# Moving each unit's predicated copy into the next unit on VectorE, and fewer masks on GpSimd, in the last tile of a fused attention and two-layer kernel

## The chip, the cores and the metric

The kernel runs on one core of a Trainium2 chip. The metric is the time of one execution on the device in microseconds (us); of the kernel before there are three runs, and one further execution was taken with the profiler.

## What is computed

Channel attention over two batches of 6016 tokens with 256 channels, then a gated layer, then a second layer with its own nonlinearity. Cut to what matters:

```python
def _moe2_ref(x, w_in, w_out):          # x: 12032 x 256, w_in: 256 x 2048, w_out: 2048 x 256
    h = x @ w_in
    g = h - np.tanh(h)
    return (g @ w_out).astype(np.float32)
```

Before it, `_attn_ref` normalises q and k along the tokens, forms a 256 x 256 softmax for each batch and applies it to v, and `_moe_ref` computes `(sigmoid(x @ w_gate) * (x @ w_val)) @ w_out`. The change touches only how `h - tanh(h)` is worked out for the last tokens.

## The kernel before, in words

**Tiles and units.** The tokens are cut into 24 tiles of up to 512 (`token_tiles`; `NT` is 24). Work comes in units: kind 1 is one of 12 slices of the gated layer of a tile, kind 2 is one of 16 slices (`K2`) of 128 hidden channels of the second layer of a tile. The list `units` is sorted by a due time. All units of kind 1 are over before the 16 units of kind 2 of the last tile (`i == NT - 1`, tile 23) begin, so those 16 follow one another with nothing between them.

**A unit of kind 2** has three parts. `s2_mm` computes the hidden values H of 128 channels in a PSUM bank (six matmuls: weights and values are split into a high and a low half, and three of the four products are taken). `s2_a` computes s = H - tanh(H). `part_b` splits s into halves: a cast on ScalarE (line 564) and a subtraction (line 566) that runs on GpSimd for the late units (`late`), on VectorE for the very last one. `part_c` multiplies the halves with the output weights (six matmuls, lines 469, 470, 474).

**The nonlinearity** in the last tile, for unit m: ScalarE computes u = H squared (line 531), d = tanh(H) (line 532) and s = (scaled u plus a bias) squared (line 533). VectorE computes e = H - d into a PSUM bank (line 543), H = H * u (line 544), s = (s + constant) * H (line 549): a polynomial that is exact enough for small H. A mask `big` says where u is over a limit, and there VectorE's predicated copy (line 550) puts e in the place of s. The mask is made by GpSimd (line 546) where m % 3 is not 0 and m is below 14, otherwise by ScalarE (line 548): nine on GpSimd, seven on ScalarE.

**Order.** Every engine works through its own queue in the order in which the program issues its instructions. In the loop over units at the end of the kernel, unit m issues `part_a` (its matmuls, then `s2_a`), then `step_b`, which is `part_b` of unit m-1, and then `part_c` of unit m-3 (`LAG` is 3). So ScalarE's queue for unit m is: square, tanh, square with bias, the mask if it is ScalarE's, the cast of unit m-1. VectorE's queue for unit m is: subtract, multiply, fused add-multiply, predicated copy. GpSimd's is: the mask if it is GpSimd's, the subtraction of unit m-1. TensorE's is: the hidden matmuls of unit m, the output matmuls of unit m-3. In unit 2 of the last tile the output matmuls and the two output copies (line 594) of tile 22 come between the unit's hidden matmuls and its `s2_a`.

**Buffers.** u, d, the mask and e have two buffers each, s has two for even and two for odd units, the PSUM ring of H has four banks, the halves (`hl`) have four.

Of the kernel before, what the change touches and what calls it, by code (L numbers as in the profile page):

```python
# [12 lines left out]
I16 = mybir.dt.int16  # L13
# [9 lines left out]
K1, K2 = F1 // P, F2 // P  # L23
# [43 lines left out]
def attn_moe_kernel(  # L67
# [12 lines left out]
    nc = tc.nc  # L80
# [15 lines left out]
    def bank(tag, name):  # L96
        return pp.tile([P, CH], F32, tag=tag, name=name)
# [423 lines left out]
    def late(i, m):  # L521
        return i == NT - 2 and m >= LATE or i == NT - 1 and m < K2 - 1

    def s2_a(i, m):
        n = tiles[i][3]
        H = live[2, i, m][:, :n]
        u = m2.tile([P, NM], F32, tag="u", bufs=2, name=f"u{i}_{m}")[:, :n]
        d = m2.tile([P, NM], F32, tag="d", bufs=2, name=f"d{i}_{m}")[:, :n]
        s = (yp if m % 2 and (i == NT - 1 or late(i, m)) else m2).tile([P, NM], F32, tag="s", bufs=2, name=f"s{i}_{m}")[:, :n]
        big = m2.tile([P, NM], BF16, tag="big", bufs=2, name=f"big{i}_{m}")[:, :n]  # L530
        nc.scalar.activation(u, H, AF.Square)  # L531
        nc.scalar.activation(d, H, AF.Tanh)  # L532
        nc.scalar.activation(s, u, AF.Square, scale=C_S, bias=c_b[:, 0:1])  # L533
        if i < NT - 1:
            nc.scalar.activation(big, u, AF.Relu, bias=c_m[:, 0:1])  # L535
            nc.vector.tensor_sub(d, H, d)  # L536
            w = H if late(i, m) else u
            nc.vector.tensor_mul(w, H, u)  # L538
            nc.vector.scalar_tensor_tensor(s, s, C_D, w, op0=ALU.add, op1=ALU.mult)  # L539
            nc.vector.copy_predicated(s, big.bitcast(I16), d)  # L540
        else:
            e = bank(f"y{m % 2}", f"e{m}")[:, :n]
            nc.vector.tensor_sub(e, H, d)
            nc.vector.tensor_mul(H, H, u)
            if m % 3 and m < K2 - 2:
                nc.gpsimd.tensor_scalar(big, u, U_MAX, 1.0, op0=ALU.is_gt, op1=ALU.mult)
            else:
                nc.scalar.activation(big, u, AF.Relu, bias=c_m[:, 0:1])
            nc.vector.scalar_tensor_tensor(s, s, C_D, H, op0=ALU.add, op1=ALU.mult)
            nc.vector.copy_predicated(s, big.bitcast(I16), e)  # L550
        live[2, i, m] = s

    def part_a(u, between=lambda: None):

        (s1_mm if u[1] == 1 else s2_mm)(*u[2:])
        between()
        (s1_a if u[1] == 1 else s2_a)(*u[2:])
# [296 lines left out]
```

## Time and profile before

| | us |
|---|---|
| median of three runs | 2313.92 |
| range of the three runs | 2313.4 to 2314.68 |
| the profiled execution's own time | 2314.18 |
| its span, first to last instruction | 2312.4 |
| busy in the span: TensorE | 2300.1 |
| busy in the span: VectorE | 1814.1 |
| busy in the span: ScalarE | 1577.3 |
| busy in the span: GpSimd | 81.2 |

In the rows below PE is TensorE, DVE is VectorE, ACT is ScalarE and POOL is GpSimd. L550 is line 550 of the kernel before. A row of a timeline has the start in us from the span's start, the duration in us, the engine, the line, the operation, what it writes and reads by the program's names, and its count; in square brackets stands how long the engine was idle before it and which instruction ended that. Durations are those of the instruction: two neighbours on one engine that do not depend on each other can overlap, so the distance of their starts is what counts. A row of stretches gives for each engine how many us of the stretch it was busy, then the granted clock of TensorE (1.00 is the higher of its two levels, 2.4 GHz), then the share and rate of the DMA engines.

### The profile page before, as it was taken

Reading aid. Unit: us, or ns where it says so; the run is one execution under the profiler, and the core shown is the slowest. Engines: PE = TensorE matmul, PEld = TensorE weight load, DVE = VectorE, ACT = ScalarE, POOL = GpSimd, SP = SyncE. Lnnn points to the kernel's source line nnn. Section 1 sums busy time; section 2 is a strip of 40 time slices with the busy share of each in tenths; the row PEclk is TensorE's granted clock in tenths of the full one; section 3 lists DMA queues with packets and bytes.
Section 4 is the critical chain, followed back from the end, with each engine's and each line's share of the span. In section 5 each row is a group of like instructions: output and inputs, shape, how many; then the busy total and the mean of one; then the engine's idle time right before and its main releaser. Section 6 shows DMA issues by size and latency. Waiting matters only on the chain.

```text
span 2312.4 us, 28293 instructions
## 1 busy us (share of the span) xinstructions
PE 2300.1 (99%) x10416; PEld 1927.1 (83%) x10416; DVE 1814.1 (78%) x2882; ACT 1577.3 (68%) x2872; POOL 81.2 (4%) x63
## 2 busy tenths in 40 slices
PE   9999999999999999999999999999999999999998
PEld 7888888888888888888899988888888888888886
DVE  5778888888888888877777777877777778777778
ACT  7567777677676767766666666666666666666667
POOL 5000000000000000000000000000000000000017
PEclk9999999999999999999999999999999999999999
DMA  9640001110101101011110000000000000000000
GB/s 341 237 134 8 23 19 37 37 37 19 37 28 32 37 19 37 0 35 35 55 37 17 10 8 19 1 19 10 10 19 10 10 19 1 19 10 10 10 1 19
DMA packets 39530, 84.65 MB, mean 37 GB/s; under 512 B 4064, under 2 KB 17376, under 8 KB 37856
## 3 DMA queue, kind: packets, MB, share of 16 engines
q1 hardware_dynamic: 38352, 76.30, 9.9%
q0 software_dynamic: 896, 6.29, 0.7%
q8 instruction: 81, 1.33, 0.2%
q14 instruction: 57, 0.47, 0.1%
q10 hardware_dynamic: 144, 0.26, 0.0%
HBM read 63.96 MB, written 18.87 MB: 36 GB/s over the span
## 4 chain that ended last, share of the span: by engine, by line
PE 94%; DVE 3%; DMA 1%; ACT 1%; issue 0%; SPq 0%; DVEq 0%; ACTq 0%
PE ps L470 11%; PE ps L469 11%; PE ps L474 11%; PE h L470 7%; PE o L474 7%; PE h L474 7%; PE h L469 7%; PE o L469 7%; PE o L470 7%; PE y L470 5%; PE y L469 5%; PE y L474 5%; DMA rawk<-in_k_dram 1%; PE aw L314 0%; PE aw L315 0%; PE aw L316 0%
## 5 line engine op out<-in xcount | busy, mean ns | idle before, releaser
L470 PE MATMUL ps<-vhl,aw 128*128 128x512 f32 (+1 forms) x1152 | 443.6, 385 | 0.0
L469 PE MATMUL ps<-vhl,aw 128*128 128x512 f32 (+1 forms) x1152 | 443.3, 385 | 0.0
L536 DVE TENSOR_TENSOR d<-h,d 128x512 f32<-128x512 f32 (+1 forms) x368 | 249.5, 678 | 235.1 <-ACT d L532 234.7
L564 ACT CAST hl<-s 128x512 fp32r<-128x512 f32 (+1 forms) x384 | 234.8, 612 | 275.1 <-DVE s L540 267.7
L531 ACT ACTIVATE u<-h 128x512 f32<-128x512 f32 (+1 forms) x384 | 226.5, 590 | 241.1 <-PE h L474 240.8
L474 PE MATMUL ps<-vhl,aw 128*128 128x512 f32 (+1 forms) x1152 | 349.8, 385 | 0.0
L538 DVE TENSOR_TENSOR u<-h,u 128x512 f32<-128x512 f32 (+1 forms) x360 | 243.5, 676 | 111.2 <-ACT big L535 111.1
L469 PE MATMUL o<-hl,wv 128*128 128x512 f32 (+1 forms) x768 | 295.8, 385 | 1.5 <-ACT hl L564 1.4
L470 PE MATMUL h<-yhl,wi 128*128 128x512 f32 (+1 forms) x768 | 295.7, 385 | 0.0
L469 PE MATMUL h<-yhl,wi 128*128 128x512 f32 (+1 forms) x768 | 295.6, 385 | 0.0
L470 PE MATMUL o<-hl,wv 128*128 128x512 f32 (+1 forms) x768 | 295.5, 385 | 0.0
L540 DVE COPY_PREDICATED s<-big,d 128x512 f32<-128x512 int16 (+1 forms) x368 | 272.8, 741 | 13.1
L533 ACT ACTIVATE s<-u,c_b 128x512 f32<-128x512 f32 (+1 forms) x384 | 275.2, 717 | 2.0 <-DVE hl L566 2.0
L535 ACT ACTIVATE big<-u,c_m 128x512 bf16<-128x512 f32 (+1 forms) x368 | 262.2, 712 | 0.0
L539 DVE SCALAR_TENSOR_TENSOR s<-s,u 128x512 f32<-128x512 f32 (+1 forms) x360 | 245.0, 681 | 12.3
L470 PEld LDWEIGHTS ps<-vhl,aw 128*128 128x128 f32 x1152 | 216.4, 188 | 40.8
L474 PEld LDWEIGHTS ps<-vhl,aw 128*128 128x128 f32 x1152 | 215.7, 188 | 41.5
L469 PEld LDWEIGHTS ps<-vhl,aw 128*128 128x128 f32 x1152 | 216.4, 188 | 40.5
L510 DVE TENSOR_TENSOR sg<-ps,sg 128x512 f32<-128x512 f32 (+1 forms) x288 | 194.3, 675 | 70.7 <-PE ps L474 55.0
L566 DVE TENSOR_TENSOR hl<-s,hl 128x512 fp32r<-128x512 f32 (+1 forms) x361 | 241.6, 669 | 0.7 <-ACT hl L564 0.7
L509 ACT ACTIVATE sg<-ps 128x512 f32<-128x512 f32 (+1 forms) x288 | 169.9, 590 | 98.0 <-PE ps L474 93.5
L474 PE MATMUL o<-hl,wv 128*128 128x512 f32 (+1 forms) x768 | 234.6, 387 | 1.8 <-POOL hl L566 1.5
(172 smaller groups left out, 3573.7 us busy)
## 6 DMA issues: line engine op xcount, KB each, us to landing
vraw<-in_vT_dram SPq DMA_DIRECT2D x22, 512.0 KB, 3.8
out_dram<-out SPq DMA_DIRECT2D x43, 256.0 KB, 2.2
raw_wgv<-in_wgv_dram SPq DMA_DIRECT2D x12, 512.0 KB, 6.7
wgv_d<-wgv POOLq DMA_DIRECT2D x6, 1024.0 KB, 7.3
wb<-wgv_d SPq DMA_DIRECT2D x6, 1024.0 KB, 4.8
raw<-in_q_dram SPq DMA_DIRECT2D x47, 128.0 KB, 2.1
raw<-in_k_dram SPq DMA_DIRECT2D x47, 128.0 KB, 2.2
rawq<-in_q_dram SPq DMA_DIRECT2D x8, 512.0 KB, 9.9
```

Of the source, the lines that this page charges most:

```text
L469: mm(ps[:, :n], wh, xh, start=first and j == 0, stop=False)
L470: mm(ps[:, :n], wl, xh, start=False, stop=False)
L474: mm(ps[:, :n], wh, xl, start=False, stop=last and j == len(wts) - 1)
L531: nc.scalar.activation(u, H, AF.Square)
L533: nc.scalar.activation(s, u, AF.Square, scale=C_S, bias=c_b[:, 0:1])
L535: nc.scalar.activation(big, u, AF.Relu, bias=c_m[:, 0:1])
L536: nc.vector.tensor_sub(d, H, d)
L538: nc.vector.tensor_mul(w, H, u)
L539: nc.vector.scalar_tensor_tensor(s, s, C_D, w, op0=ALU.add, op1=ALU.mult)
L540: nc.vector.copy_predicated(s, big.bitcast(I16), d)
L564: nc.scalar.copy(hl[:, 0, :n], x)
L566: eng.tensor_sub(hl[:, 1, :n], x, hl[:, 0, :n].bitcast(F32))
```

## The change

Two edits in `s2_a`, both for the last tile alone.

- The predicated copy is no longer issued at the end of its own unit. It is put in a list as a function, and the next unit issues it after its own subtract and multiply and just before its own fused add-multiply. The last unit issues its own copy at its end.
- GpSimd makes the mask of the odd units below 15 (seven masks), ScalarE those of the even units and of unit 15 (nine).

```diff
@@ -521,6 +521,8 @@
     def late(i, m):
         return i == NT - 2 and m >= LATE or i == NT - 1 and m < K2 - 1
 
+    choose = []
+
     def s2_a(i, m):
         n = tiles[i][3]
         H = live[2, i, m][:, :n]
@@ -542,12 +544,16 @@
             e = bank(f"y{m % 2}", f"e{m}")[:, :n]
             nc.vector.tensor_sub(e, H, d)
             nc.vector.tensor_mul(H, H, u)
-            if m % 3 and m < K2 - 2:
+            if m % 2 and m < K2 - 1:
                 nc.gpsimd.tensor_scalar(big, u, U_MAX, 1.0, op0=ALU.is_gt, op1=ALU.mult)
             else:
                 nc.scalar.activation(big, u, AF.Relu, bias=c_m[:, 0:1])
+            if choose:
+                choose.pop()()
             nc.vector.scalar_tensor_tensor(s, s, C_D, H, op0=ALU.add, op1=ALU.mult)
-            nc.vector.copy_predicated(s, big.bitcast(I16), e)
+            choose.append(lambda: nc.vector.copy_predicated(s, big.bitcast(I16), e))
+            if m == K2 - 1:
+                choose.pop()()
         live[2, i, m] = s
```

The cast of unit m-1 (`part_b`) is still issued in unit m after `s2_a` of unit m, so it follows the moved copy in the program.

## Rows read from the trace of the kernel before

**Rows 1.** The page, busy time of each engine over the span, share and instructions.
```profile
PE 2300.1 (99%) x10416; PEld 1927.1 (83%) x10416; DVE 1814.1 (78%) x2882; ACT 1577.3 (68%) x2872; POOL 81.2 (4%) x63
```

**Rows 2.** Stretches of 10 us, one of the last tile; the first line names the columns.
```profile
core 0: us, PE busy (x) PEld busy (x) DVE busy (x) ACT busy (x) POOL busy (x), PEclk, DMA share, GB/s
2280.00:2290.00 10.00, 10.00 (x45) 8.03 (x44) 9.38 (x15) 8.36 (x16) 9.24 (x6) 1.00 0.00 0
```

**Rows 3.** The chain that ended last, 2250 to 2313 us, shares by engine and line.
```profile
by line: DVE s L550 16.6%; DVE s L549 15.5%; DVE h L544 11.5%; DVE e L543 11.2%; issue 5.9%; ACT hl L564 5.9%; ACT u L531 5.6%; ACT s L533 3.9%; DVE s L540 3.0%; ACT out L594 2.6%; ACT d L532 1.8%; ACT yhl L101 1.7%; ACT big L548 1.6%; PE o
```

**Rows 4.** Timeline of VectorE, one round of the last tile.
```profile
2283.09 0.70 DVE L543 TENSOR_TENSOR e<-h,d 128x512 f32<-128x512 f32 x1
2283.70 0.69 DVE L544 TENSOR_TENSOR h<-h,u 128x512 f32<-128x512 f32 x1
2284.49 0.69 DVE L549 SCALAR_TENSOR_TENSOR s<-s,h 128x512 f32<-128x512 f32 x1
2285.29 0.75 DVE L550 COPY_PREDICATED s<-big,e 128x512 f32<-128x512 int16 x1
2285.93 0.70 DVE L543 TENSOR_TENSOR e<-h,d 128x512 f32<-128x512 f32 x1
```

**Rows 5.** Timeline of ScalarE in the same round.
```profile
2283.24 0.62 ACT L564 CAST hl<-s 128x512 fp32r<-128x512 f32 x1 [0.62 <-DVE s L550]
2283.76 0.59 ACT L531 ACTIVATE u<-h 128x512 f32<-128x512 f32 x1
2284.25 0.59 ACT L532 ACTIVATE d<-h 128x512 f32<-128x512 f32 x1
2284.73 0.72 ACT L533 ACTIVATE s<-u,c_b 128x512 f32<-128x512 f32 x1
2285.34 0.72 ACT L548 ACTIVATE big<-u,c_m 128x512 bf16<-128x512 f32 x1
2286.07 0.62 ACT L564 CAST hl<-s 128x512 fp32r<-128x512 f32 x1
```

**Rows 6.** Timeline, tile 22: a subtract of VectorE that waited for its tanh.
```profile
2245.15 0.59 ACT L532 ACTIVATE d<-h 128x512 f32<-128x512 f32 x1
...
2245.77 0.69 DVE L536 TENSOR_TENSOR d<-h,d 128x512 f32<-128x512 f32 x1 [2.56 <-ACT d L532]
```

**Rows 7.** Timelines of VectorE and ScalarE, first units of the last tile.
```profile
2261.88 0.69 DVE L549 SCALAR_TENSOR_TENSOR s<-s,h 128x512 f32<-128x512 f32 x1 [0.46 <-ACT d L532]
...
2263.44 0.62 ACT L564 CAST hl<-s 128x512 fp32r<-128x512 f32 x1 [0.95 <-DVE s L550]
2263.97 1.06 ACT L594 COPY out<-o 128x512 f32<-128x512 f32 x2
2264.92 0.61 ACT L531 ACTIVATE u<-h 128x512 f32<-128x512 f32 x1
...
2266.12 0.70 DVE L543 TENSOR_TENSOR e<-h,d 128x512 f32<-128x512 f32 x1
```

**Rows 8.** Groups by line from 2262 us on: GpSimd's two operations, busy, mean ns, idle.
```profile
L566 POOL TENSOR_TENSOR hl<-s,hl 128x512 fp32r<-128x512 f32 x16 | 20.7, 1294 | 6.8 <-ACT hl L564 4.5 <-issue 1.6
L546 POOL TENSOR_SCALAR big<-u 128x512 bf16<-128x512 f32 x9 | 17.3, 1922 | 0.8
```

**Rows 9.** Timeline of TensorE: output of unit 0, hidden of units 9, 10, 15.
```profile
2264.60 0.50 PE L469 MATMUL o<-hl,wv 128*128 128x512 f32 x1 [0.16 <-ACT out L594]
...
2281.35 0.39 PE L469 MATMUL h<-yhl,wi 128*128 128x512 f32 x1
...
2284.07 0.39 PE L469 MATMUL h<-yhl,wi 128*128 128x512 f32 x1
...
2298.19 0.39 PE L469 MATMUL h<-yhl,wi 128*128 128x512 f32 x1
```

**Rows 10.** Timelines of VectorE and TensorE: subtract and output of unit 15.
```profile
2302.89 0.70 DVE L543 TENSOR_TENSOR e<-h,d 128x512 f32<-128x512 f32 x1
...
2306.52 0.49 PE L469 MATMUL o<-hl,wv 128*128 128x512 f32 x1 [0.66 <-ACT hl L564]
```

**Rows 11.** A stretch near the end, columns as in the first stretch above.
```profile
2303.70:2306.50 2.80, 1.94 (x6) 0.97 (x6) 1.91 (x3) 0.62 (x1) 1.29 (x1) 1.00 0.00 0
```

## The prediction

> **What bounds the kernel now.** I read four views in this order. First the page's busy times: TensorE is busy 99% of the span [rows 1], so over the kernel as a whole only TensorE's order matters, and a change on VectorE counts only where TensorE is not last. Second the stretches of 10 us: in the last tile VectorE has risen to 9.38 of 10 us and GpSimd to 9.24 [rows 2]. Third the chain of waits of the last 60 us: its largest shares are VectorE's four lines of the second layer, 550, 549, 544 and 543 [rows 3]. In order of time that chain is VectorE alone from 2271 to 2306 us. Fourth the timeline of VectorE: a round of one unit is subtract, multiply, fused add-multiply, predicated copy, and the next subtract comes 2285.93 - 2283.09 = 2.84 us after the last [rows 4]. The starts tell where the round goes. Subtract to multiply takes 0.61 us, though the subtract lasts 0.70: the two do not depend on each other and overlap. Multiply to fused operation and fused operation to copy take 0.79 and 0.80, though these last only 0.69: each needs the result just before it, and 0.1 us passes first. Copy to the next subtract takes 0.64 (0.75 long, overlapped). So VectorE sets the pace of 2.83 to 2.84 us, TensorE's own is 2284.07 - 2281.35 = 2.72 [rows 9], and the price of the two dependent pairs is visible: about 0.18 us each against an independent neighbour.
>
> **The other side of the round.** ScalarE works in the order of the program: square, tanh, square with bias, perhaps the mask, then the cast of the unit before, and only then the square of the next unit [rows 5]. The cast waits for the predicated copy (0.62 us idle, released by line 550). From the end of a copy to the end of the next unit's tanh there is a fixed chain: 0.03 to the cast (copy 2285.29 + 0.75 = 2286.04, cast 2286.07 [rows 4, 5]), 0.52 from the cast to the square, 0.49 to the tanh, 0.59 for the tanh [rows 5]. The subtract needs that tanh; where it waited for one, it started 0.03 us after it (2245.15 + 0.59 = 2245.74, then 2245.77 [rows 6]). From a copy's start this makes 0.75 + 0.03 + 0.52 + 0.49 + 0.59 + 0.03 = 2.41 us to the earliest subtract of the unit after next. In the kernel before, the copy of unit m-1 and the subtract of unit m+1 lie 0.64 + 2.84 = 3.48 us apart on VectorE, so this chain has 1.07 us to spare and never shows. That slack is what the change uses.
>
> **The change, part by part.**
>
> (a) The copy moves. VectorE's new order is subtract(m), multiply(m), copy(m-1), fused(m). No instruction is added or removed. Now each dependent pair has another instruction between it. No row shows multiply followed by a copy that does not need it; the nearest rows are 0.61 (subtract to multiply) and 0.64 (copy to subtract) below and 0.79 (dependent pair) above. I take 0.61, because the operand of the copy is long done. VectorE alone would then go round in about 0.61 + 0.61 + 0.64 + 0.61 = 2.47 us, 0.37 less.
>
> (b) What waits for the moved copy. The cast of unit m-1 on ScalarE now waits for a copy that stands behind subtract(m) and multiply(m). Behind the cast on ScalarE are square(m+1) and tanh(m+1), and for that tanh waits subtract(m+1), behind which are multiply(m+1) and copy(m). This closes a loop from copy(m-1) to copy(m): 2.41 us to the subtract, 0.61 to the multiply, 0.61 to the copy, together 3.63 us a unit. That is more than VectorE's 2.84 and TensorE's 2.72, so ScalarE and VectorE take turns and VectorE idles about 3.63 - 2.47 = 1.16 us a unit. With 0.79 for the multiply-to-copy step it is 3.81; if each of its eight steps is read 0.01 too long, it is 3.55.
>
> (c) The masks. GpSimd makes seven (units 1, 3, ... 13) instead of nine, ScalarE nine instead of seven. A mask takes 1.92 us on GpSimd [rows 8] and pushes ScalarE's next instruction by about 0.61 to 0.72 [rows 5]. In the new round ScalarE has finished square, tanh, square and mask 0.49 + 0.48 + 0.61 + 0.72 = 2.30 us after it began; the copy that the cast waits for ends at 0.49 + 0.59 + 0.03 + 0.61 + 0.61 + 0.75 = 3.08. So the mask is hidden by 0.8 us of waiting; without that cover the two extra masks cost at most 2 x 0.72 = 1.4 us. On GpSimd two rounds need 1.92 + 2 x 1.29 = 4.5 us of 7.26 [rows 8]; its masks are due a whole round later, so GpSimd drops out as a limit. No DMA is issued in the loop of units.
>
> (d) The first rounds. Unit 0 keeps its place to the fused operation at 2261.88 [rows 7]. Then subtract(1) at 2262.49, multiply(1) at 2263.10, copy(0) at 2263.71 to 2264.46, cast(0) at 2264.49 instead of 2263.44: 1.05 us late. The two output copies of the tile before and square(2) follow it on ScalarE [rows 7], so square(2) moves from 2264.92 to 2265.97, its tanh ends 1.08 later, and subtract(2) starts at 2267.08 instead of 2266.12.
>
> (e) The rounds from subtract(2) to subtract(15): 13 x 3.63 = 47.2, so subtract(15) starts at 2314.3 instead of 2302.89 [rows 10]: 11.4 us later.
>
> (f) The tail. Before, the last product (unit 15) began 2306.52 - 2302.89 = 3.63 us after subtract(15) [rows 10]. Now copy(14) ends 0.61 + 0.61 + 0.75 = 1.97 after it, the cast ends at 2.62 (0.03 and 0.62), GpSimd's subtraction at 3.95 (1.29 and about 0.04 to start), and TensorE still has two matmuls of unit 14 (2 x 2.72 / 12 = 0.45) ahead of unit 15: 4.44. The path through unit 15's own copy, 0.61 + 0.61 + 0.64 + 0.80 = 2.66 and then 0.75 + 0.03 + 0.62 + 0.04, gives 4.10 and is covered. So the tail is 0.8 us longer.
>
> Sum: 11.4 + 0.8 = 12.2 us. The profiled execution took 2314.18 us (span 2312.4 and 1.8 around it); the median shown is 2313.92, 0.3 lower. That gives 2326.4 on the profiled one and 2326.1 on the median; I write 2326.3, which is 0.53% slower.
>
> **One rule of the notes.** VectorE's rows show independent neighbours starting 0.61 to 0.64 us apart although the first lasts 0.70 to 0.75 [rows 4]. The Trainium skill, page "VectorE: DVE Perf Modes", section "The DRAIN you can't avoid", says that the next operation does not start until the pipeline has emptied and that eight copies took the same time with a semaphore after each as with one at the end. By that rule separating the dependent pairs gains nothing, and the sum would be that of the second rival below. The trace disagrees for these operations: it has two distances, not one.
>
> **Rivals.**
>
> The gain is kept (not slower). Mechanism: the wait of the cast does not hold back the next unit, VectorE falls to 2.47 and TensorE's 2.72 takes over. Place: the step cast(m-1) to square(m+1) on ScalarE. It decides as soon as the loop of 3.63 falls below 2.84, that is if 0.8 us of it is not there. Price: the product of unit 0 (2264.60 [rows 9]) starts 1.05 later for the cast; from there the hidden product of unit 15 comes 1.36 + 11 x 2.72 = 31.3 later, at 2296.9 instead of 2298.19 [rows 9]. Subtract(15) can follow 1.36 + 0.03 + 0.49 + 0.59 + 0.03 = 2.5 after that, at 2299.4 instead of 2302.89, and the tail gives back 0.8: 2.7 us faster, 2311.5, which is 0.12% and no measurable change. For it speaks only that VectorE is the chain today; against it every row of ScalarE, where the square never starts before the cast ahead of it. Chance 5%.
>
> The moved copy costs a dependent step. Multiply to copy takes 0.79: 3.81 a round, 13 x 0.18 = 2.3 more and 0.2 in the tail, 2328.8. Chance 6%.
>
> TensorE's clock falls. In the new round TensorE works 2.72 of 3.63 us and pauses in each. At half the granted clock, the 1.2 GHz level, a unit would cost 5.44 us and bound the stretch: 13 x 1.81 = 23.5 more, about 2350. It decides only if the grant leaves 1.00 (the 2.4 GHz level). Against it: from 2303.7 to 2306.5 TensorE was busy 1.94 of 2.80 us, and the grant stayed at 1.00 [rows 11]. Chance 3%.
>
> The change does nothing that shows, because the copy lands where it was or the loop has as much slack as before: 2314, chance 3%.
>
> **How the numbers follow.** The forecast (the loop of 3.63) has 83%; the predicted time is its own, 2326.3. Its bounds: 13 x 0.08 = 1.0 and the tail's 0.8 and the start's 1.0 down if these are hidden, 0.2 of spread below the median: 2323.3. Up: the dependent step's 2.5, spread 0.8 above the median and 0.4 for slower instructions: 2330. The range 2323.3 to 2330 holds the forecast and the second rival. A measurement of this kernel can tell about 0.2%, 4.6 us, from no change. Slower by more: the forecast, the second and the third rival, 92%. Within: the first and the last rival but for a point, 7%. Faster by more needs 4.6 us where the first rival has 2.7: 1%.
>
> **What would show it.** In the profile after, on VectorE multiply, copy, fused start 0.61 and 0.64 apart, and 1.1 to 1.2 us of idle time stands before each subtract, released by the tanh (line 532). ScalarE's cast waits 0.8 to 1.5 us for the copy in every unit. Subtract to subtract is 3.6, TensorE waits in each unit with the grant at 1.00, and the chain alternates between cast, square, tanh and subtract, multiply, copy. If the round is below 2.84 the loop was wrong; at 3.8 the copy's step was.

## The result and the profile after

| | us |
|---|---|
| median of the kernel before (five runs) | 2313.56 |
| median of the kernel after (five runs, 2325.75 to 2328.48) | 2326.86 |
| ratio, with its 95% interval | 1.0056 (1.0045 to 1.0067) |
| the profiled execution after | 2325.75 |
| its span | 2324.0 |

The change makes the kernel 0.56% slower, some 13 us. Between the two profiled executions the loss lies in the last tile: the span grew by 11.6 us, and the last product of the tile moved from 2306.52 [rows 10] to 2318.18, by 11.7. Two executions among the experiments, one of the masks alone (3886.91 us, mean granted clock 0.556) and one of the kernel before (2874.96 us, 0.753), are left out of the ratios below, though not of the medians.

In the rows of the kernel after, the lines have moved: VectorE's subtract is L545, its multiply L546, the fused operation L553, the predicated copy L554; ScalarE's square is L533, the tanh L534, the square with bias L535, the mask L550 and the cast L570; GpSimd's subtraction is L572.

First the stretch that answers to [rows 2], with the same columns.

```profile
2280.00:2290.00 10.00, 9.09 (x34) 5.94 (x35) 6.71 (x11) 7.30 (x14) 5.79 (x4) 1.00 0.01 2
```

VectorE fell from 9.38 to 6.71 us of 10, ScalarE from 8.36 to 7.30, GpSimd from 9.24 to 5.79, TensorE from 10.00 to 9.09. Every engine is less busy, and the work takes longer: the sign of engines that wait for one another in turn. One round of VectorE, which answers to [rows 4]:

```profile
2284.68 0.70 DVE L545 TENSOR_TENSOR e<-h,d 128x512 f32<-128x512 f32 x1 [1.11 <-ACT d L534]
2285.29 0.69 DVE L546 TENSOR_TENSOR h<-h,u 128x512 f32<-128x512 f32 x1
2285.89 0.73 DVE L554 COPY_PREDICATED s<-big,e 128x512 f32<-128x512 int16 x1
2286.51 0.67 DVE L553 SCALAR_TENSOR_TENSOR s<-s,h 128x512 f32<-128x512 f32 x1
...
2288.30 0.70 DVE L545 TENSOR_TENSOR e<-h,d 128x512 f32<-128x512 f32 x1 [1.11 <-ACT d L534]
```

The four operations now start 0.61, 0.60 and 0.62 us apart: both steps of 0.8 are gone, as the change means them to be. But before every subtract VectorE stands idle for 1.11 us until the tanh. ScalarE over the same round, which answers to [rows 5]:

```profile
2286.66 0.62 ACT L570 CAST hl<-s 128x512 fp32r<-128x512 f32 x1 [1.40 <-DVE s L554]
2287.18 0.59 ACT L533 ACTIVATE u<-h 128x512 f32<-128x512 f32 x1
2287.67 0.59 ACT L534 ACTIVATE d<-h 128x512 f32<-128x512 f32 x1
2288.15 0.72 ACT L535 ACTIVATE s<-u,c_b 128x512 f32<-128x512 f32 x1
2288.76 0.72 ACT L550 ACTIVATE big<-u,c_m 128x512 bf16<-128x512 f32 x1
2290.27 0.62 ACT L570 CAST hl<-s 128x512 fp32r<-128x512 f32 x1 [0.79 <-DVE s L554]
```

The cast waits 1.40 us for the copy in a unit without a mask on ScalarE, 0.79 in one with a mask, and the next square cannot start before the cast. So a mask on ScalarE only fills a wait. The chain that ended last, one round of its pieces (start, us, what):

```profile
2291.91 0.70 DVE e L545
2292.61 0.60 DVE h L546
2293.20 0.65 DVE s L554
2293.85 0.02 issue
2293.88 0.62 ACT hl L570
2294.50 0.50 ACT u L533
2295.00 0.49 ACT d L534
```

Where the chain before was VectorE alone from 2271 to 2306 us, it now runs from VectorE to ScalarE and back once a unit. Last the waits over the tile, in us in total, times and the longest; the first line is of the kernel before, the other two of the kernel after.

```profile
ACT hl L564 <- DVE s L550: 7.3, 9, 2.2
```

```profile
ACT hl L570 <- DVE s L554: 17.4, 16, 2.0
DVE e L545 <- ACT d L534: 16.5, 14, 2.1
```

The wait of the subtract for the tanh does not appear at all in this view of the kernel before, so all 16.5 us of it are new.

### The profile page after: what moved, and what is told of

It reads as the page before. It is cut to its first block, busy times and chain, and to the rows that moved or that the text cites. A ratio compares the mean times of both kernels' runs of the same rounds, so it can differ in the third digit from the quotient of the medians.

```text
span 2324.0 us, 28299 instructions
## 1 busy us (share of the span) xinstructions
PE 2306.6 (99%) x10416; PEld 1926.2 (83%) x10416; DVE 1812.1 (78%) x2882; ACT 1579.3 (68%) x2874; POOL 77.3 (3%) x61
## 4 chain that ended last, share of the span: by engine, by line
PE 93%; DVE 2%; ACT 2%; DMA 1%; issue 1%; SPq 0%; POOLq 0%; DVEq 0%; ACTq 0%
PE ps L470 11%; PE ps L469 11%; PE ps L474 11%; PE o L474 7%; PE h L470 7%; PE h L474 7%; PE h L469 7%; PE o L470 7%; PE o L469 7%; PE y L470 5%; PE y L469 5%; PE y L474 5%; DMA rawk<-in_k_dram 1%; PE aw L314 0%; PE aw L315 0%
## 5 line engine op out<-in xcount | busy, mean ns | idle before, releaser
L570 ACT CAST hl<-s 128x512 fp32r<-128x512 f32 (+1 forms) x384 | 234.8, 612 | 285.5 <-DVE s L542 268.1
L533 ACT ACTIVATE u<-h 128x512 f32<-128x512 f32 (+1 forms) x384 | 226.5, 590 | 240.5 <-PE h L474 240.2
L535 ACT ACTIVATE s<-u,c_b 128x512 f32<-128x512 f32 (+1 forms) x384 | 275.9, 718 | 2.0 <-DVE hl L572 2.0
L572 DVE TENSOR_TENSOR hl<-s,hl 128x512 fp32r<-128x512 f32 (+1 forms) x361 | 241.7, 669 | 0.7 <-ACT hl L570 0.7
```

The source lines that it names most:

```text
L570: nc.scalar.copy(hl[:, 0, :n], x)
L572: eng.tensor_sub(hl[:, 1, :n], x, hl[:, 0, :n].bitcast(F32))
```

## The experiments

Three theories were set against each other. A: the moved copy closes a loop (copy, cast, square, tanh, subtract, multiply, next copy), and its length is the round. B: the two masks that went from GpSimd to ScalarE cost the time. C: the halves come too late for TensorE's product three units on. The ratios are against the kernel before in runs on the same chip.

**Each part of the change alone.** The masks alone (the copy as before):

```diff
-            if m % 3 and m < K2 - 2:
+            if m % 2 and m < K2 - 1:
```

> The copy stays where the kernel before has it; only the masks are dealt out anew (seven on GpSimd, nine on ScalarE). Theory A, the loop copy - cast - square - tanh - subtract - multiply - copy: the loop is not closed, VectorE still sets the pace with 2.83 us a unit, and the time is that of the kernel before, 2313.6 within 1.5 us. Theory B, the two masks more on ScalarE are what costs: most of the 13 us, some 2326. Theory C, the halves come too late for TensorE's product three units on: 2313.6 as well, for the copy is not late here.

Measured: 2313.93, ratio 0.9998 (0.9989 to 1.0008). The move alone, which is the kernel after with the old line for the masks:

> The copy is moved, the masks are dealt out as in the kernel before (nine on GpSimd). Theory A: the loop is closed as in the kernel after, 3.61 us a unit, 2326 to 2328. Theory B: 2311 to 2314, since the masks are back. Theory C: 2326 to 2328.

Measured: 2326.59, ratio 1.0053 (1.0041 to 1.0066). The whole of the loss is the move's; the masks cost nothing that the runs can tell in either order. B falls.

**The dose.** If the length of the loop is the round, taking an instruction out from ahead of the copy must shorten the round by that instruction's step, and putting one in must lengthen it. The copy between subtract and multiply:

```diff
             nc.vector.tensor_sub(e, H, d)
+            if choose:
+                choose.pop()()
             nc.vector.tensor_mul(H, H, u)
...
-            if choose:
-                choose.pop()()
             nc.vector.scalar_tensor_tensor(s, s, C_D, H, op0=ALU.add, op1=ALU.mult)
```

> As the kernel after, but the copy of the unit before is issued between the subtract and the multiply, so one instruction of 0.61 us less stands ahead of it. Theory A: the loop is 2.41 + 0.61 = 3.02 us, and this is the distance from subtract to subtract in the trace; against the kernel after 13 x 0.59 = 7.7 us less in the rounds, 0.6 less at the start, 0.4 less at the end: 2317 to 2319. VectorE alone would need 0.61 + 0.63 + 0.79 + 0.61 = 2.64. Theory B: no change against the kernel after, 2327. Theory C: the halves come 0.6 us earlier of the 1.2 us that they are late, so about half of the loss stays, 2320, with a round that follows TensorE's waits and not the 3.02.

Measured: 2317.98, ratio 1.0016 (1.0007 to 1.0025). VectorE's timeline, one round (here the multiply is L548):

```profile
2279.39 0.70 DVE L545 TENSOR_TENSOR e<-h,d 128x512 f32<-128x512 f32 x1 [0.29 <-ACT d L534]
2279.99 0.73 DVE L554 COPY_PREDICATED s<-big,e 128x512 f32<-128x512 int16 x1
2280.61 0.70 DVE L548 TENSOR_TENSOR h<-h,u 128x512 f32<-128x512 f32 x1
2281.42 0.69 DVE L553 SCALAR_TENSOR_TENSOR s<-s,h 128x512 f32<-128x512 f32 x1
2282.39 0.70 DVE L545 TENSOR_TENSOR e<-h,d 128x512 f32<-128x512 f32 x1 [0.29 <-ACT d L534]
```

Subtract to subtract is 3.00 us, and the wait for the tanh has shrunk from 1.11 to 0.29. The copy behind the fused operation:

```diff
-            if choose:
-                choose.pop()()
             nc.vector.scalar_tensor_tensor(s, s, C_D, H, op0=ALU.add, op1=ALU.mult)
+            if choose:
+                choose.pop()()
             choose.append(lambda: nc.vector.copy_predicated(s, big.bitcast(I16), e))
```

> As the kernel after, but the copy of the unit before is issued after the unit's fused operation, so a dependent step of 0.80 us more stands ahead of it. Theory A: the loop is 2.41 + 0.60 + 0.80 + 0.60 = 4.41 us, read from subtract to subtract; 13 x 0.80 = 10.4 us more than the kernel after in the rounds, 0.8 more at the start and at the end: 2337 to 2340. TensorE then works 2.72 of 4.41 us. If its granted clock falls to the 1.2 GHz level in these pauses, a unit costs it 5.44 us and the time goes to 2350 or more. If the late copy as such costs a fixed sum and not a loop, the time stays near 2327.

Measured: 2339.61, ratio 1.0113 (1.0098 to 1.0129).

```profile
2273.10 0.70 DVE L545 TENSOR_TENSOR e<-h,d 128x512 f32<-128x512 f32 x1 [1.67 <-ACT d L534]
...
2275.11 0.72 DVE L554 COPY_PREDICATED s<-big,e 128x512 f32<-128x512 int16 x1
2277.50 0.70 DVE L545 TENSOR_TENSOR e<-h,d 128x512 f32<-128x512 f32 x1 [1.67 <-ACT d L534]
```

The round is 4.40 us. In all three orders the stretch from the copy's start to the next subtract is the same: 2.41 us in the kernel after (2285.89 to 2288.30), 2.40 and 2.39 here. Only what stands between subtract and copy differs: 1.21 in the kernel after (2284.68 to 2285.89), 0.60 and 2.01 here. That sum is the round: 3.62, 3.00 and 4.40.

**The loop opened.** The copy stays where the change puts it; the cast and the subtraction of halves go behind the tanh of the following unit:

```diff
         nc.scalar.activation(d, H, AF.Tanh)
+        while casts:
+            part_b(casts.pop(0))
...
         u = qb.pop(0)
-        part_b(u)
+        if u[1:3] == (2, NT - 1) and u[3] < K2 - 1:
+            casts.append(u)
+        else:
+            while casts:
+                part_b(casts.pop(0))
+            part_b(u)
```

> As the kernel after, but the cast and the subtraction of halves of unit m-1 are issued in unit m+1 behind the tanh, instead of at the end of unit m. Theory A: the wait of the cast no longer stands ahead of the next square and tanh, the loop is open, VectorE falls to 2.47 us a unit and TensorE's 2.72 us sets the pace: 2310 to 2313. Theory B: 2327. Theory C: the halves come about 1 us later still, so the time is that of the kernel after or more, 2327 to 2340.

Measured: 2313.29, ratio 0.9996 (0.9988 to 1.0005). With the loop opened the loss is gone, and A holds. The number is 0.3 above the range that was expected. Against C this run says less than was expected of it: the halves come later only in the program's order. In time the cast of unit 7 starts 5.29 us behind its subtract (2278.26 to 2283.55), and 5.59 us in the kernel after (2284.68 to 2290.27). What speaks against C stands in the trace of the kernel after. The hidden values of unit 15 are the last ones that TensorE makes; they are ready 3.57 us before ScalarE's square begins on them:

```profile
2308.24 0.62 PE L474 MATMUL h<-yhl,wi 128*128 128x512 f32 x2
2312.43 0.59 ACT L533 ACTIVATE u<-h 128x512 f32<-128x512 f32 x1
```

No square of that tile waits for TensorE, so late products cannot have set the round, and C falls. In the run with the loop opened the waits say what took over:

```profile
ACT u L533 <- PE h L474: 4.0, 6, 1.0
PEld o L474 <- POOL hl L574: 3.9, 7, 0.7
```

ScalarE now waits for TensorE, which is the pace that was expected, but TensorE itself waits now and then for GpSimd's subtraction, which stands behind a mask. To see whether that is what keeps it from 2.72 us, GpSimd got only every fourth mask (`if m % 4 == 1`):

> As cast_later, but GpSimd makes only the masks of units 1, 5, 9 and 13. In cast_later the rounds were 2.83 us on average: TensorE's 2.72 and, every few units, 0.2 to 0.3 us in which it waited for GpSimd's subtraction behind a mask of 1.92 us. If GpSimd's masks are what keeps cast_later from TensorE's pace, the rounds go to 2.72 to 2.76 and the time to 2311.5 to 2313. If ScalarE takes over as the limit (2.74 us in units with a mask), the round stays near 2.8 and the time at 2313.

Measured: 2313.62, ratio 0.9995 (0.9986 to 1.0003).

```profile
2278.33 0.73 PE L474 MATMUL o<-hl,wv 128*128 128x512 f32 x2 [0.26 <-POOL hl L574]
2281.59 0.70 DVE L547 TENSOR_TENSOR e<-h,d 128x512 f32<-128x512 f32 x1 [0.69 <-ACT d L534]
2284.31 0.70 DVE L547 TENSOR_TENSOR e<-h,d 128x512 f32<-128x512 f32 x1 [0.21 <-ACT d L534]
2289.66 0.73 PE L474 MATMUL o<-hl,wv 128*128 128x512 f32 x2 [0.15 <-POOL hl L574]
2292.92 0.70 DVE L547 TENSOR_TENSOR e<-h,d 128x512 f32<-128x512 f32 x1 [0.59 <-ACT d L534]
```

Seven of the 13 rounds are now TensorE's pace (2.71 or 2.72), but from unit 2 to unit 15 the mean is still 2.79 (2264.84 to 2301.14). Two rounds hold nearly all of the excess: unit 8 started 3.20 us after unit 7, and unit 12 3.11 after unit 11, together 0.87 of the 0.94 us by which the 13 rounds exceed 13 x 2.72. Just ahead of both, TensorE waited for a subtraction of GpSimd that stood behind a mask, those of units 5 and 9. So the trace puts the excess down to the masks that GpSimd still makes; a version without any was not run. The runs do not tell these two versions apart, nor either from the kernel before. Keeping the gain on VectorE is worth less than can be measured.

**Another way to shorten the loop, which missed.** The product needs the square and not the tanh, so it was put first, with the copy behind it:

```diff
-            nc.vector.tensor_sub(e, H, d)
-            nc.vector.tensor_mul(H, H, u)
+            nc.vector.tensor_mul(e, H, u)
...
+            nc.vector.tensor_sub(H, H, d)
-            nc.vector.scalar_tensor_tensor(s, s, C_D, H, op0=ALU.add, op1=ALU.mult)
-            choose.append(lambda: nc.vector.copy_predicated(s, big.bitcast(I16), e))
+            nc.vector.scalar_tensor_tensor(s, s, C_D, e, op0=ALU.add, op1=ALU.mult)
+            choose.append(lambda: nc.vector.copy_predicated(s, big.bitcast(I16), H))
```

> As the kernel after, but VectorE's order is product of H and u (now written to the second bank), copy of the unit before, subtract of the tanh (now in place in H), fused operation. The product needs the square only, not the tanh. Theory A: the loop runs from the copy to the cast, the square and the product, 0.75 + 0.03 + 0.52 + 0.59 + 0.03 + 0.61 = 2.53 us, which is less than TensorE's 2.72, so TensorE sets the pace: 2310.5 to 2312.5, some 15 us below the kernel after and 1 to 3 us below the kernel before. If what costs is not the loop but that the copy comes after two instructions of the next unit as such, or that the halves come late for TensorE, nothing is won: 2324 to 2327.

Measured: 2316.64, ratio 1.0013 (1.0004 to 1.0022). Timelines of ScalarE and VectorE; the row of L545 is the product:

```profile
2273.84 0.59 ACT L534 ACTIVATE d<-h 128x512 f32<-128x512 f32 x1
...
2274.46 0.70 DVE L545 TENSOR_TENSOR e<-h,u 128x512 f32<-128x512 f32 x1 [0.50 <-ACT d L534]
```

The product started 0.03 us after the tanh ended, though it does not read its result. Both read the same PSUM bank, H, and the trace names the tanh as what released the product; the subtract behind it shows no wait of its own. The Trainium skill, page "PSUM — Partial Sum Buffer", section "PSUM bank collisions raise a hardware error", says that two engines must not access one bank in the same partitions at the same time, reads included, and that software has to keep them apart. The trace agrees as far as the two reads do not overlap; that this is why the product waits is so far only a reading. The size of the loss fits it: the loop kept the tanh, 2.41 + 0.60 = 3.01, and the round was 3.01. The theory's sum was right for the loop that the program has; the loop that was assumed was the wrong one. To test that reading, the product was issued ahead of the tanh, so that the tanh waits for it:

```diff
             nc.scalar.activation(u, H, AF.Square)
+            nc.scalar.activation(s, u, AF.Square, scale=C_S, bias=c_b[:, 0:1])
+            nc.vector.tensor_mul(e, H, u)
...
             nc.scalar.activation(d, H, AF.Tanh)
```

> As product_first, but the product is issued ahead of the tanh, and ScalarE's order is square, square with bias, mask, tanh, cast. In product_first the product started 0.03 us after each tanh, and the subtract behind it had no wait of its own: the program orders the two engines' reads of the bank of H, so the product waited for the tanh and not for the square. Here it can only wait for the square, and the tanh waits for the product. If that is why product_first missed, theory A gives a loop of 2.53 to 2.56 us in odd units and 2.90 in even ones (mask ahead of the tanh, then subtract and fused operation ahead of the next product): 2.73 on average, about TensorE's 2.72; 2311.5 to 2314. If the copy behind an instruction of the next unit costs in itself, the round stays at 3.0 as in product_first, 2316 to 2318.

Measured: 2314.99, ratio 1.0006 (0.9996 to 1.0015), 1 us above what was expected. Three starts of the product on VectorE, and one of the tanh on ScalarE:

```profile
2281.03 0.69 DVE L546 TENSOR_TENSOR e<-h,u 128x512 f32<-128x512 f32 x1
2281.76 0.60 ACT L551 ACTIVATE d<-h 128x512 f32<-128x512 f32 x1 [0.20 <-DVE e L546]
2283.59 0.69 DVE L546 TENSOR_TENSOR e<-h,u 128x512 f32<-128x512 f32 x1
2286.68 0.69 DVE L546 TENSOR_TENSOR e<-h,u 128x512 f32<-128x512 f32 x1
```

The wait has turned round: here the tanh, which needs nothing of the product, starts 0.04 us after it, and the product no longer waits for the tanh. The odd units go round in 2.56 us, the number that was expected, but not by the loop that was expected: the next product stands right behind the subtract and the fused operation, and that subtract starts 0.03 us after its tanh (2282.39). The even ones, with a mask ahead of the tanh, take 3.09 instead of 2.90: there the sum left out that the square with bias now follows the square that it needs, 0.69 us from start to start instead of 0.49. The reading of product_first holds, and the order gains nothing.

**TensorE's clock.** Of the five executions of the kernel after, the profiled one has a mean granted clock of 1.000 and 2325.75 us; the other four have 0.998 or 0.999 and 2326.8 to 2328.5. The kernel was run twice more to see where the clock goes.

> The kernel after once more, to see where TensorE's mean granted clock of 0.998 comes from, which four of its five executions show beside 1 to 3 us more than the one at 1.000. If it comes from the first 20 us, where TensorE waits for its inputs, the rounds of the last tile stay at 3.61 us and the last products at full speed. If it comes from the pauses of the last tile, stretches there show a clock below 1.00.

> The same once more, with the same two readings of the clock: a fall in the first 20 us, or in the pauses of the last tile.

Measured: 2325.89 and 2329.35. Stretches of the first of the two, with the columns of [rows 2]:

```profile
2310.00:2312.50 2.50, 1.08 (x4) 0.30 (x2) 2.39 (x4) 1.73 (x4) 0.47 (x1) 1.00 0.00 0
2312.50:2315.00 2.50, 2.26 (x6) 1.80 (x6) 1.40 (x4) 2.38 (x5) 1.29 (x1) 0.56 0.00 0
2315.00:2317.50 2.50, 1.80 (x6) 0.67 (x4) 1.94 (x3) 1.04 (x2) 1.09 (x1) 0.76 0.00 0
```

And two matmuls of the product of unit 13 in its slow stretch, from the timeline of TensorE:

```profile
2313.29 0.63 PE L470 MATMUL o<-hl,wv 128*128 128x512 f32 x1
2313.72 0.63 PE L469 MATMUL o<-hl,wv 128*128 128x512 f32 x1
```

After the last hidden product TensorE has only the output matmuls left, about 1.4 us of work (half of 2.72) in a round of 3.6, and there the grant fell to the lower level: matmuls start 0.43 us apart instead of 0.23. Why it fell is not shown: the profiled execution has the same order of work there, and its grant stayed.

```profile
2310.00:2312.50 2.50, 0.92 (x3) 0.30 (x2) 2.44 (x4) 1.73 (x4) 0.31 (x1) 1.00 0.00 0
```

In the first repeat the slow ones were over before the halves of unit 14 came, and nothing was lost; in the second one the slow stretch came later (matmuls start 0.43 us apart from 2320.9 on) and held up the last products: there the product of unit 15 took 1.71 us from its first matmul to the last pair, where it took 0.92 in the profiled execution. That second execution also reached the last tile 2.3 us later than the profiled one. Its grant had been 0.53 from 46 to 48 us and 0.62 from 48 to 50, and TensorE started 13 matmuls in these 4 us where the profiled execution started 22. So both readings were right in part, though the early fall came after the first 20 us. A fall in the first 20 us was seen once, in the run with the copy second:

```profile
12.00:15.00 3.00, 3.00 (x9) 2.37 (x8) 1.62 (x3) 2.22 (x4) 2.84 (x3) 0.50 1.04 419
```

There TensorE had been busy only 0.86 us of the 2 us ahead of that stretch, while it waited for its inputs. But in the second repeat it was busy 0.68 us from 8 to 10, and the grant stayed at 1.00. In the run with the copy last the grant fell inside the rounds as well, with hidden products still to come: 0.67 and 0.64 in the two stretches of 2.5 us from 2267.5 on, behind a wait of 1.97 us. The rounds kept their 4.40 us, and from 2272.5 to 2325 the grant was 1.00, though TensorE paused in every round. Executions of the kernel before show a lower mean too: of the 27 beside the first four experiments, eight have a mean clock of 0.999 and take 2315.3 to 2316.7 us, the other 19 have 1.000 and 2313.2 to 2314.8. Where the clock fell in those was not profiled, and how often it falls in the last tile of the kernel after was not counted. The median of the kernel after lies 1.1 us above the profiled execution; how much of that is the clock's is not shown.

## Why the prediction was right

The forecast was 2326.3 us, slower by 0.53%; measured were 2326.86 and 0.56%. Step by step:

- **What bounds the kernel, and the slack of 1.07 us on the other side of the round.** Right: this was the step on which everything hung. The chain of waits of before named VectorE alone from 2271 to 2306 us, and did not show how near the chain through ScalarE was. It had to be added up from starts that no wait stood ahead of.
- **(a) The copy's step.** Right: 0.60 behind the multiply, 0.62 to the fused operation, where 0.61 and 0.64 were taken. The dependent steps of 0.79 are gone, so the second rival falls: independent neighbours start before the one ahead has ended (0.60 to 0.62 apart, 0.67 to 0.73 long). The rule that the prediction set beside it was quoted in part. The section "The DRAIN you can't avoid" of the page "VectorE: DVE Perf Modes" of the Trainium skill also says that a next operation which is not held starts earlier, and the trace agrees with that.
- **(b) The loop.** Right: from subtract(2) at 2266.66 to subtract(15) at 2313.55 there are 13 rounds of 3.61 us, where 3.63 were taken. The idle time ahead of the subtract is 1.11 (1.16 forecast).
- **(c) The masks.** Right: hidden by a wait that is 0.79 us where a mask is made, and the run with the masks alone shows no cost that it can tell. The remark that no DMA is issued in the loop is not so: the outputs of tile 22 leave in unit 2 (DMA share 0.15 from 2260 to 2270 us, before and after alike); nothing in the sum rests on it.
- **(d) The start.** Right: the last tile began 0.41 us earlier in the profiled execution after (the fused operation of unit 0 at 2261.47 instead of 2261.88), and subtract(2) at 2266.66 is 2267.08 less that.
- **(f) The tail.** The path was right, the size 0.2 short: from subtract(15) to the last product 4.63 us instead of 4.44. The terms that were mis-sized are TensorE's pair of matmuls of unit 14, which takes 0.58 us behind a wait, not 0.45, and GpSimd's start, 0.13 us after the cast and not 0.04. (The terms as written, 3.95 and 0.45, make 4.40; 4.44 has another 0.04, for TensorE's start, which took 0.06.)

```profile
2315.50 0.62 ACT L570 CAST hl<-s 128x512 fp32r<-128x512 f32 x1 [0.77 <-DVE s L554]
...
2316.25 1.29 POOL L572 TENSOR_TENSOR hl<-s,hl 128x512 fp32r<-128x512 f32 x1 [2.36 <-issue]
...
2317.60 0.74 PE L474 MATMUL o<-hl,wv 128*128 128x512 f32 x2 [0.23 <-POOL hl L572]
2318.18 0.39 PE L469 MATMUL o<-hl,wv 128*128 128x512 f32 x1
```

The profiled execution took 2325.75, 0.7 below the sum of 2326.4 that was made for it: about 0.4 of that is the earlier start of the tile and 0.3 the 13 rounds, and the tail gives 0.2 back. The median lies 0.8 above the 2326.1 of the forecast; the clock is the likely reason, but the executions around the median were not profiled. The two deviations have opposite signs, so that the median came within 0.6 us of 2326.3 is in part luck. The loop's size is not: 3.61 against 3.63.

Of the rivals, the one in which the gain is kept had the right point of decision: with the loop opened the time did go to the kernel before's side, at 2313.3 where 2311.5 had been worked out, since the rounds came to 2.83 on average and not to 2.72. The rival of the clock was put too simply. It priced a fall that lasts through the whole tile, and dismissed it by a single stretch at 1.00; the two repeats show falls of some microseconds in the last units, after the hidden products are over, which cost nothing in one and about 1.2 us in the other. The rounds up to 2310 us stood at 1.00 in all three profiles.

## What to carry to other kernels

An instruction that is moved later on one engine is also later for whoever waits for it, and for everything behind that waiter in its queue; follow the wait until it comes back to the moved instruction, and add up the loop. The chain that ended last shows only the longest of several loops: before a change that shortens it, work out the next one from the starts of instructions that waited for nothing. Here VectorE's own work in a round fell from 2.83 us to 2.50 (3.61 less 1.11 idle). Between a copy and the next subtract it has 1.30 us of work left, and the chain through ScalarE reaches that subtract only 2.41 us after the copy; the difference is the idle time that the trace shows.

## What the runs showed of the hardware that was not expected

- A product on VectorE waited for a tanh on ScalarE whose result it does not use, because both read one PSUM bank; it started 0.03 us after the tanh. With the order turned round the tanh waited for the product (0.04 us after its end).
- TensorE's granted clock fell to a mean of 0.56 over 2.5 us behind a stretch with 1.08 us of matmuls in 2.5, and held at 1.00 behind the same stretch with 0.92 us of them in another execution of the kernel after. So one stretch at 1.00, like that of 1.94 us busy in 2.80 [rows 11] on which the prediction relied, does not show that the grant will hold; what decides it is not shown.
- A pair of matmuls behind a wait takes 0.58 us to the next matmul (2317.60 to 2318.18), against 0.45 in an unbroken run.
